# Windowed attention and a squared-ReLU MoE: reciprocals kept for a range test, with a second path behind a branch

## The chip, the core and the metric

The kernel runs on one core of a Trainium2 chip. The metric is the device time of one execution in microseconds; of a kernel several executions are timed, and the median is given. One further execution is recorded by the hardware profiler: its span runs from the first to the last instruction that the profile shows.

The engines are named as the profile names them: PE is TensorE (matrix multiplies; PEld its weight loads), DVE is VectorE, ACT is ScalarE, POOL is GpSimd and SP is SyncE. A "q" behind a name (SPq, ACTq) marks the engine's own sequencer: DMA issues, semaphore waits, drains. Each engine runs its own list of instructions in order; between engines they wait for each other through semaphores.

## The reference, cut to what matters

```python
# q, k, v: [8 batches, 8 heads, 576 positions, 64], float32, randn * 0.1
scores = scale * np.matmul(q, k.transpose(0, 1, 3, 2))        # scale = 1/8
mask = np.abs(pos[:, None] - pos[None, :]) <= 32
scores = np.where(mask, scores, -1e9)
scores = scores - np.max(scores, axis=-1, keepdims=True)
attn = np.exp(scores)
attn = attn / (np.sum(attn, axis=-1, keepdims=True) + 1e-09)
x = np.matmul(attn, v)          # heads side by side: [4608 tokens, 512]
r = np.maximum(x @ w_in, 0.0)   # w_in: [512, 2048]
out = (r * r) @ w_out           # w_out: [2048, 512]; out: [4608, 512] float32
```

## The kernel before, in words

The kernel works in bfloat16 with float32 accumulation, and it leaves out the row maximum: the exponentials are taken of the scores as they are.

*Tiles.* The 4608 tokens are cut into 24 groups G of 192 queries, three to a batch. A group has two halves, w = 0 (A) and w = 1 (B), each with 128 keys by 128 queries for 8 heads. `scores` (L565) puts transposed scores of one half into PSUM (`at`), ScalarE takes the exponential (L586, L589), VectorE multiplies by a mask of zeros and ones (L594). `pv` (L622) multiplies by v, which has a column of ones beside its 64 columns, so that column 64 of each head is the sum of the exponentials. On VectorE, the reciprocal of these sums (L641) goes into one of four small buffers `rs` (128 partitions by 8 heads), and a multiply (L644) with `rs` spread along 64 columns writes the normalised output into `xa` or `xb`. Half A uses partitions 64 to 127 alone, half B all 128. `xturn` transposes the outcome into `xt`: the first three groups on TensorE, the others by transposing DMAs that SyncE issues (L717, L720).

*MoE.* `mm1` (L737) multiplies `xt` with `w_in` into one of two PSUM tiles `ht`; ScalarE takes the relu (L743) into one of four buffers `rt`; VectorE squares (L746) into `gt`. `mm2` (L757) multiplies 128 tokens of `gt` with `w_out` into `outp`, ScalarE copies to `oe` (L767) and issues the store (L769). The last 128 tokens go in three column pieces (`mm2_last`, L782, L789, L792, L795); ScalarE issues two of their stores and SyncE one.

*Loads.* GpSimd issues the loads of q, k, v and the weights (L394, L426, L443, L456, L461), as they change type. Only the first two loads (L407) are SyncE's. In the opening TensorE fills its waits with multiplies of zeros (L322).

*What sets the order.* Nothing is issued as it is written. `Prog.rec` notes each operation with its engine, what it reads and writes, an estimated duration and a key; `Prog.schedule` simulates the engines with these durations and lets each engine take, of what is ready, the operation with the lowest key. `Prog.emit` writes the lists in the order found and adds a wait where an operation needs one of another engine, or an earlier result of its own. Operations of one engine that only reuse a buffer get no wait. Keys count steps of 64 tokens: group G has the keys 3G - 13 and a little more, `mm1` of tokens from t0 on has t0/64 to t0/64 + 8, `mm2` of block u has 2u + 9 to 2u + 10.5.

*The end.* `emit` runs in one block (L873). Behind the last operation SyncE waits for the landings of all stores (L877), and the block closes with a barrier of all engines: each drains and reports, GpSimd collects the reports and releases all.

The functions that the change touches:

Of the kernel before, what the change touches and what calls it, by code (L numbers as in the profile page):

```python
# [6 lines left out]
ACTF = mybir.ActivationFunctionType  # L7
BF16 = mybir.dt.bfloat16
F32 = mybir.dt.float32

B_, H_, S_, D_ = 8, 8, 576, 64
DM = 512
# [70 lines left out]
class Prog:  # L83
# [148 lines left out]
    def emit(self):  # L232
        nc = self.nc
        engs = {"PE": nc.tensor, "ACT": nc.scalar, "DVE": nc.vector, "POOL": nc.gpsimd, "SP": nc.sync}
        for op in self.ops:
            for d in op.deps:
                if d.dma is None and not (d.eng == "PE" and op.eng == "PE"):
                    d.inc = True
        sems = {e: nc.alloc_semaphore(f"s_{e}") for e in engs}
        count = {e: 0 for e in engs}  # L240
        dsems, dcount, total = {}, {}, {}
        for op in self.ops:
            if op.dma is not None:
                total[op.dma] = dcount[op.dma[0]] = dcount.get(op.dma[0], 0) + 16
        waited = {}
        for op in self.ops:
            e = engs[op.eng]
            need = {}
            for d in op.deps:
                if d.dma is None and d.eng == "PE" and op.eng == "PE":  # L250
                    continue
                need[d.sem] = max(need.get(d.sem, 0), d.val)
            for s, v in need.items():
                if waited.get((op.eng, s), 0) >= v:
                    continue
                waited[(op.eng, s)] = v
                e.wait_ge(sems[s] if s in sems else dsems[s], v)
            ins = op.fn(e)
            if op.dma is not None:
                s = op.dma[0]  # L260
                if s not in dsems:
                    dsems[s] = nc.alloc_semaphore(f"d_{s}")
                op.sem, op.val = s, total[op.dma]
                ins.then_inc(dsems[s], 16)
            elif op.inc:
                count[op.eng] += 1
                op.sem, op.val = op.eng, count[op.eng]
                ins.then_inc(sems[op.eng], 1)
        return dsems, dcount
# [10 lines left out]
class Gen:  # L280
# [5 lines left out]
    def alloc(self):  # L286
        nc = self.nc
        sb, ps = nc.alloc_sbuf_tensor, nc.alloc_psum_tensor
        self.AT = ps("at", [128, 2048], F32)
        self.HT = [ps(f"ht{i}", [128, 512], F32) for i in range(2)]  # L290
        self.OUTP = [ps(f"outp{i}", [128, 512], F32) for i in range(2)]

        self.RAW = {t: [sb(f"{t}raw{i}", [128, 2, 512], BF16) for i in range(NRAW)] for t in "qk"}
        self.QT = [sb(f"qt{i}", [128, 4, S_], BF16) for i in range(2)]
        self.KT = [sb(f"kt{i}", [128, 4, KW], BF16) for i in range(2)]
        self.V = [sb(f"v{i}", [128, 2, H_, VS], BF16) for i in range(NV)]
        self.DIF = sb("dif", [128, 128], F32)
        self.MASK = [sb(f"mask{i}", [128, 128], BF16) for i in range(4)]
        self.ID = sb("ident", [128, 128], BF16)
        self.E = [sb(f"e{i}", [128, 1024], BF16) for i in range(2)]  # L300
        self.PT = [sb(f"pt{i}", [128, 8, 128], BF16) for i in range(3)]
        self.RS = [sb(f"rs{i}", [128, 8], F32) for i in range(4)]
        self.XA = [sb(f"xa{i}", [128, 512], BF16) for i in range(3)]
        self.XB = [sb(f"xb{i}", [128, 512], BF16) for i in range(3)]
        self.XT = sb("xt", [128, 4, RING], BF16)
        self.W1 = sb("w1", [128, 4, DFF], BF16)
        self.W2 = sb("w2", [128, 16, DM], BF16)
        self.GT = sb("gt", [128, 16, RING], BF16)
        self.RT = [sb(f"rt{i}", [128, 512], BF16) for i in range(4)]
# [288 lines left out]
    def pv(self, G, w):  # L598
        b, g = divmod(G, 3)
        n = 2 * G + w  # L600
        key = 3 * G - LEAD + 0.3 * w + 0.1
        reg = 1 if NBIAS <= G < NSPLIT or G < NDUP and w else 0
        c0 = 1024 * reg
        vt, pt, avp = self.V[G % NV], self.PT[n % 3], self.AT
        hi, lo = [self.half(2 * reg, x) + self.half(2 * reg + 1, x) for x in (1, 0)]


        def f(e):
            if w and G < NDUP:
                for h in range(8):  # L610
                    x, y = divmod(h, 4)
                    c = c0 + 512 * x + 65 * y
                    e.matmul(avp[:, c:c + 65], self.PT[(n - 1) % 3][:, 4 * (h % 2) + h // 2, :], vt[:, 0, h, 0:65], start=(y == 0),
                             stop=True, skip_group_check=True)
            if w and G < NCLR:
                for x in range(2):
                    e.matmul(avp[64:128, c0 + 512 * x + 508:c0 + 512 * x + 512], self.ZZ[:, 0:64], self.ZZ[:, 0:4], start=True,
                             stop=True, skip_group_check=True)
            for h in range(8):
                x, y = divmod(h, 4)  # L620
                c = c0 + 512 * x + 65 * y
                mm = e.matmul(avp[:, c:c + 65], pt[:, 4 * (h % 2) + h // 2, :], vt[:, w, h, 0:65], start=(w == 0 and y == 0),  # L622
                              stop=True, skip_group_check=True)
            return mm

        rd = [("v", G % NV, w), ("vset", G % NV), ("pt", n % 3), "zz"]
        if G % 3 != 1:
            rd.append(("vpad", G % NV))
        if g and w == 0 and G < NVR:
            rd.append(("vl", G % NV))  # L630
        if G < NDUP and w:
            rd += [("pt", (n - 1) % 3), ("v", G % NV, 0)]
        self.p.rec("PE", f, reads=rd + (lo if w and G >= NDUP else []), writes=hi + lo, key=key, dur=260 + 160 * (w and G < NCLR) + 260 * (w and G < NDUP),
                   name=f"P{G}{'AB'[w]}")
        r0 = 64 * (1 - w)
        rs = self.RS[n % 4]
        x = (self.XB if w else self.XA)[G % 3]
        rd = hi + lo if w else hi
        av = avp[r0:128, c0:c0 + 1024].rearrange("p (x c) -> p x c", x=2)[:, :, 0:260].rearrange("p x (y c) -> p x y c", y=4)
        m = 128 - r0  # L640
        self.p.rec("DVE", lambda e: e.reciprocal(rs[r0:128, :].rearrange("p (x y) -> p x y", x=2), av[:, :, :, 64]),  # L641
                   reads=rd, writes=[("rs", n % 4)], key=key - 0.05, dur=190, name=f"R{G}{'AB'[w]}")
        rb = bass.AP(rs, r0 * 8, [[8, m], [4, 2], [1, 4], [0, 64]])
        self.p.rec("DVE", lambda e: e.tensor_tensor(x[r0:128, :].rearrange("p (x y c) -> p x y c", x=2, y=4),  # L644
                                                    av[:, :, :, 0:64], rb, ALU.mult),
                   reads=rd + [("rs", n % 4)], writes=[("xb" if w else "xa", G % 3)], key=key - 0.05,
                   dur=dve(512, False), name=f"N{G}{'AB'[w]}")
# [151 lines left out]
    def build(self):  # L799
# [37 lines left out]
        def at(key, f, *a):  # L837
            todo.append((key, len(todo), f, a))
# [20 lines left out]
        while t0 < NTOK:  # L859
            n = FIRST[t0] if t0 in FIRST else 192 if t0 < 768 else 256 if t0 < T512 else 512  # L860
            m = min(512 // n, 4)
            for d in range(0, 16, m):
                key = t0 / 64 + d / 16 * n / 64
                at(key, self.mm1, t0, n, list(range(d, d + m)), key)
            t0 += n
        at(500, self.mm2_last, NBLK - 1, 500)
        for u in range(NBLK - 1):
            for seg in range(4):
# [3 lines left out]
        p.schedule()  # L872
        with self.nc.Block():  # L873
            dsems, dcount = p.emit()
            for s in dsems:
                if s[0] == "o":
                    self.nc.sync.wait_ge(dsems[s], dcount[s])  # L877

    def opening(self):
        return OPENING  # L880


def bass_sliding_window_symmetric__then__act_relu_squared_kernel(nc, q, k, v, moe_w_in, moe_w_out, out):
# [29 lines left out]
```

## Time and profile before

| | |
|---|---|
| timed runs | 301.8, 302.01 and 302.15 us; median 302.01 us |
| profiled execution | span 299.9 us; a time of its own beside the span is not given |
| HBM | 36.70 MB read, 9.44 MB written |
| first matmul of the MoE (L737) in the span | 17.46 us |
| last reciprocal (L641) | 240.58 us |
| last matmul (L782) ends | 297.6 us |
| last store issued | 297.98 us |

How to read it: the page gives each engine's busy time, then the span in 40 slices with the busy share of each in tenths, the DMA queues, the chain of work that ended last, and groups of instructions. A group's row has line, engine, operation, output<-inputs, size and count, then its busy time and the mean in ns of one, then the idle time of the engine just before and what ended it. A row of the timeline has start in us, duration in us, engine, line and operation; in brackets stands the idle time before it and who ended it. A row for one line has the shortest, median and longest duration in ns and the first and last start in us.

### The profile page before, as it was taken

To read this page: it belongs to the slowest core of one execution; us is meant where nothing else is said; L and a number is where in the kernel's file an instruction comes from. 1 tells how busy PE (TensorE), PEld (TensorE's weight loads), DVE (VectorE), ACT (ScalarE), POOL (GpSimd) and SP (SyncE) were. 2 spreads that over 40 slices of the span, in tenths; PEclk is the share of its full clock that TensorE was granted. 3 is DMA by queue.
4 is the path that set the end of the run, shared out by engine and by line. 5 is a ranking of instruction groups with operands and counts; after the bars stand their busy time and mean duration, and the time that the engine had idled before them with its cause. 6 is when DMAs were issued, how large, how long until landed. Compare 5 with 4: busy or idle time off the path is not lost.

```text
span 299.9 us, 6209 instructions
## 1 busy us (share of the span) xinstructions
PE 291.9 (97%) x2394; PEld 171.8 (57%) x2431; DVE 167.2 (56%) x385; ACT 160.3 (53%) x250; POOL 107.1 (36%) x143
## 2 busy tenths in 40 slices
PE   7899999999999999999999999999999999999996
PEld 3578866848677767664544454444544444444445
DVE  6898775737674767563656666665666632222100
ACT  3497834836467656750765476536744643443312
POOL 8993336503544354455256335533500000000000
PEclk9999999999999999999999999999999999999999
DMA  9999999997999999999999999999992120100112
GB/s 169 176 206 184 196 177 174 169 176 137 164 169 165 95 162 146 155 138 186 180 168 131 114 166 156 125 149 156 154 128 70 55 61 35 37 35 35 38 70 105
DMA packets 160636, 39.83 MB, mean 133 GB/s; under 512 B 149984, under 2 KB 156128, under 8 KB 160608
## 3 DMA queue, kind: packets, MB, share of 16 engines
q0 software_dynamic: 106016, 17.93, 89.3%
q1 hardware_dynamic: 49264, 12.14, 28.5%
q10 hardware_dynamic: 5328, 9.37, 9.1%
q8 instruction: 19, 0.31, 0.5%
q14 instruction: 9, 0.07, 0.1%
HBM read 36.70 MB, written 9.44 MB: 154 GB/s over the span
## 4 chain that ended last, share of the span: by engine, by line
PE 90%; DMA 5%; POOL 3%; issue 1%; ACT 0%; POOLq 0%; ACTq 0%
PE ht L737 41%; PE outp L757 40%; DMA w<-in_moe_w_in_dram 5%; PE at L622 4%; PE at L565 4%; POOL v L443 1%; POOL w L456 1%; PE at L485 1%; PE ht L782 1%; PE outp L782 1%; POOL kpair L426 1%; POOL qpair L426 1%; ACT rt L743 0%; ACT oe L792 0%; POOL dif L325 0%
## 5 line engine op out<-in xcount | busy, mean ns | idle before, releaser
L737 PE MATMUL ht<-xt,w 128*128 128x256 bf16 (+2 forms) x885 | 140.0, 302 | 1.3 <-DMA w<-in_moe_w_in_dram 0.5
L757 PE MATMUL outp<-w,gt 128*128 128x512 bf16 x536 | 133.0, 379 | 1.3
L743 ACT ACTIVATE rt<-ht 128x512 bf16<-128x512 f32 (+1 forms) x152 | 85.9, 578 | 87.1 <-PE ht L737 85.1
L737 PEld LDWEIGHTS ht<-xt,w 128*128 128x128 bf16 x896 | 81.3, 98 | 43.8 <-ACT rt L743 0.6
L746 DVE TENSOR_TENSOR gt<-rt 128x512 bf16<-128x512 bf16 (+1 forms) x152 | 61.5, 408 | 61.6 <-ACT rt L743 60.0
L757 PEld LDWEIGHTS outp<-w,gt 128*128 128x128 bf16 x560 | 51.9, 98 | 54.1 <-ACT oe L767 1.0
L394 POOL DMA_DIRECT2D kraw<-in_k_dram x36 | 27.7, 778 | 107.3 <-PE at L622 56.8
L589 ACT ACTIVATE e<-at 128x1024 bf16<-128x1024 f32 x46 | 44.8, 1021 | 8.7 <-PE at L565 8.4
L594 DVE TENSOR_TENSOR pt<-e,mask 128x1024 bf16<-128x1024 bf16 x46 | 31.8, 691 | 29.0 <-ACT e L589 28.9
L443 POOL DMA_DIRECT2D v<-in_v_dram x48 | 38.2, 809 | 0.0
L767 ACT ACTIVATE oe<-outp 128x512 f32<-128x512 f32 x35 | 21.1, 604 | 29.6 <-PE outp L757 29.6
L394 POOL DMA_DIRECT2D qraw<-in_q_dram x36 | 27.7, 778 | 0.0
L622 PEld LDWEIGHTS at<-v,pt 128*128 128x128 bf16 x384 | 18.3, 98 | 9.9 <-DMA v<-in_v_dram 0.6
L622 PE MATMUL at<-v,pt 128*128 128x65 bf16 x384 | 20.1, 194 | 0.5 <-ACT pt L586 0.5
L644 DVE TENSOR_TENSOR xa<-at,rs 64x512 bf16<-64x512 f32 x24 | 16.7, 695 | 0.9
L644 DVE TENSOR_TENSOR xb<-at,rs 128x512 bf16<-128x512 f32 x24 | 16.5, 689 | 0.7
L565 PEld LDWEIGHTS at<-qt,kt 64*128 64x128 bf16 x384 | 10.8, 94 | 8.7 <-issue 7.1
L565 PE MATMUL at<-qt,kt 64*128 64x128 bf16 x384 | 15.2, 217 | 0.2
L641 DVE RECIPROCAL rs<-at 64x8 f32<-64x8 f32 (+1 forms) x48 | 10.0, 209 | 9.1 <-PE at L622 7.7
L650 DVE MEMSET at<- 64x520 f32 x23 | 11.3, 492 | 3.5 <-DVE xa L644 2.6
L450 DVE COPY v<-v 64x512 bf16<-64x512 bf16 x16 | 5.9, 372 | 5.1 <-PE ht L737 2.9
L789 DVE COPY oe<-ht 128x128 f32<-128x128 f32 x1 | 0.3, 292 | 14.5 <-PE ht L782 14.5
(67 smaller groups left out, 83.2 us busy)
## 6 DMA issues: line engine op xcount, KB each, us to landing
out_dram<-oe ACTq DMA_DIRECT2D x35, 256.0 KB, 3.2
qraw<-in_q_dram POOLq DMA_DIRECT2D x36, 96.0 KB, 5.8
w<-in_moe_w_in_dram POOLq DMA_DIRECT2D x4, 512.0 KB, 10.7
v<-in_v_dram POOLq DMA_DIRECT2D x16, 128.0 KB, 6.6
w<-in_moe_w_out_dram POOLq DMA_DIRECT2D x4, 512.0 KB, 18.8
v<-in_v_dram POOLq DMA_DIRECT2D x16, 96.0 KB, 7.0
kraw<-in_k_dram POOLq DMA_DIRECT2D x12, 112.0 KB, 4.6
kraw<-in_k_dram POOLq DMA_DIRECT2D x12, 96.0 KB, 4.9
```

Source lines behind the costliest of these rows:

```text
L394: self.p.rec("POOL", lambda e, j=j: e.dma_start(raw[0:h, j, :].rearrange("p (h d) -> p h d", h=8), s[:, j]), writes=[("raw", t, G % NRAW, ...
L443: self.p.rec("POOL", lambda e, j=j, lo=lo, hi=hi, k0=k0: e.dma_start(vt[lo - k0:hi - k0, j, :, 0:64], self.v[b, :, lo:hi, :].rearrange("h ...
L565: mm = e.matmul(sc[:, 512 * par + 128 * j:512 * par + 128 * j + 128], kt[r:r + 64, j, k0:k0 + 128], q, start=G >= NBIAS, stop=True, skip_g ...
L589: self.p.rec("ACT", lambda e, e_=e_, sc=sc: e.activation(e_[:], sc, ACTF.Exp, scale=0.125), reads=tags[w], writes=[("e", n % 2)], key=key, ...
L594: self.p.rec("DVE", lambda e, pt=pt, ee=ee, mb=mb: e.tensor_tensor(pt[:], ee, mb, ALU.mult), reads=[("e", n % 2), ("mask", mi)], writes=[( ...
L622: mm = e.matmul(avp[:, c:c + 65], pt[:, 4 * (h % 2) + h // 2, :], vt[:, w, h, 0:65], start=(w == 0 and y == 0), stop=True, skip_group_chec ...
L644: self.p.rec("DVE", lambda e: e.tensor_tensor(x[r0:128, :].rearrange("p (x y c) -> p x y c", x=2, y=4), av[:, :, :, 0:64], rb, ALU.mult), ...
L737: mm = e.matmul(ht[:, n * x:n * x + n], self.W1[:, ft, 128 * d:128 * d + 128], self.XT[:, ft, r:r + n], start=(ft == 0), stop=(ft == 3))
L743: self.p.rec("ACT", lambda e: e.activation(rt[:, 0:c], ht[:, 0:c], ACTF.Relu), reads=[f"ht{k % 2}"], writes=[("rt", k % 4)], key=key, dur= ...
L746: self.p.rec("DVE", lambda e: e.tensor_tensor(gt[:, d0:d0 + len(ds), r:r + n], rr, rr, ALU.mult), reads=[("rt", k % 4)], writes=[("gt", s, ...
L757: mm = e.matmul(op[:], gt[:, d, r:r + 128], self.W2[:, d, :], start=(d == 0), stop=(d == 15))
L767: self.p.rec("ACT", lambda e: e.activation(oe, op[:], ACTF.Copy), reads=[f"outp{u % 2}"], writes=[("oe", u % 4)], key=key, dur=act(512), n ...
```

## The change

The four buffers `rs` become one tensor `rsa` with a place of its own for each of the 48 halves. A memset fills what half A does not write (partitions 0 to 63) with ones. Behind the last half, VectorE tests all 384 values of each partition against 2^-40 and 2^40 and takes the minimum; SyncE moves the 128 minima into one partition by a DMA; VectorE takes their minimum and writes a flag (0 or 1). At the end of the block all five engines wait for that instruction, load the flag into a register, and behind the barrier each compares it with 0. If it isn't 0, they enter `General`, a second path: float32 attention with row maxima in loops over batch, head and 96 queries, written to `out`, and then the MoE from `out` in a loop over 36 blocks. If it is 0, they jump over that path, which stands last in the program.

The diff, with the second path cut to its head:

```diff
-        sems = {e: nc.alloc_semaphore(f"s_{e}") for e in engs}
+        sems = self.sems = {e: nc.alloc_semaphore(f"s_{e}") for e in engs}
...
-        self.RS = [sb(f"rs{i}", [128, 8], F32) for i in range(4)]
+        self.RSA = sb("rsa", [128, 2 * NG, 8], F32)
+        self.OK = sb("ok", [128, 2 * NG * 8], F32)
+        self.OKP = sb("okp", [128, 1], F32)
+        self.OKR = sb("okr", [1, 128], F32)
+        self.OK1 = sb("okmin", [1, 1], F32)
+        self.FLAG = sb("flag", [1, 1], I32)
...
-        rs = self.RS[n % 4]
+        rs = self.RSA[:, n, :]
...
-        self.p.rec("DVE", lambda e: e.reciprocal(rs[r0:128, :].rearrange("p (x y) -> p x y", x=2), av[:, :, :, 64]),
-                   reads=rd, writes=[("rs", n % 4)], key=key - 0.05, dur=190, name=f"R{G}{'AB'[w]}")
-        rb = bass.AP(rs, r0 * 8, [[8, m], [4, 2], [1, 4], [0, 64]])
+        self.p.rec("DVE", lambda e: e.reciprocal(rs[r0:128].rearrange("p (x y) -> p x y", x=2), av[:, :, :, 64]),
+                   reads=rd, writes=[("rs", n)], key=key - 0.05, dur=190, name=f"R{G}{'AB'[w]}")
+        rb = bass.AP(self.RSA, (r0 * 2 * NG + n) * 8, [[16 * NG, m], [4, 2], [1, 4], [0, 64]])
...
+        self.range_ones()
+        at(3 * NG, self.range_flag)
...
             dsems, dcount = p.emit()
+            for e in (self.nc.tensor, self.nc.scalar, self.nc.vector, self.nc.gpsimd, self.nc.sync):
+                e.wait_ge(p.sems["DVE"], self.flagged.val)
+            off = self.nc.values_load(self.FLAG[:], min_val=0, max_val=1, ...)
             for s in dsems:
                 if s[0] == "o":
                     self.nc.sync.wait_ge(dsems[s], dcount[s])
+        with self.nc.If(off != 0):
+            General(self).build()
+
+    def range_ones(self):
+        ones = self.RSA[0:64].rearrange("p (g w) h -> p g w h", w=2)[:, :, 0, :]
+        self.p.rec("DVE", lambda e: e.memset(ones, 1.0), writes=["rsones"], key=6, dur=350, name="rsones")
+
+    def range_flag(self):
+        p, rsa = self.p, self.RSA[:].rearrange("p n h -> p (n h)")
+        key = 3 * NG
+        p.rec("DVE", lambda e: e.tensor_scalar(self.OK[:], rsa, 2.0 ** -40, None, ALU.is_ge),
+              reads=["rsones"] + [("rs", n) for n in range(2 * NG)], writes=["ok0"], key=key, dur=560, name="okge")
+        p.rec("DVE", lambda e: e.scalar_tensor_tensor(self.OK[:], rsa, 2.0 ** 40, self.OK[:], ALU.is_le, ALU.mult),
+              reads=["ok0"], writes=["ok1"], key=key, dur=560, name="okle")
+        p.rec("DVE", lambda e: e.tensor_reduce(self.OKP[:], self.OK[:], mybir.AxisListType.X, ALU.min),
+              reads=["ok1"], writes=["okp"], key=key, dur=560, name="okmin")
+        p.rec("SP", lambda e: e.dma_start(self.OKR[:], self.OKP[:]), reads=["okp"], writes=["okr"], dma=("ok", 0), key=key,
+              dur=600, move=(1, 100), name="okdma")
+        p.rec("DVE", lambda e: e.tensor_reduce(self.OK1[:], self.OKR[:], mybir.AxisListType.X, ALU.min),
+              reads=["okr"], writes=["ok2"], key=key, dur=250, name="okrow")
+        self.flagged = p.rec("DVE", lambda e: e.tensor_scalar(self.FLAG[:], self.OK1[:], 0.5, None, ALU.is_lt),
+                             reads=["ok2"], writes=["flag"], key=key, dur=100, name="flag")
+        self.flagged.inc = True
...
+class General:
+    def do(self, e, f, inc=1):
+        if self.n:
+            e.wait_ge(self.sem, self.n)
+        f(e).then_inc(self.sem, inc)
+        self.n += inc
...
+        with nc.Fori(0, B_) as b:
+            with nc.Fori(0, H_) as h:
...
+                with nc.Fori(0, N) as c:
...
+        with nc.Fori(0, NBLK) as t:
...
```

The lists of the changed program hold, on VectorE, the memset between the copy of `kt` (L516, 768 elements) and the first reciprocal, then the two tests and the reduction around the first square (L746) behind the last multiply (L644), and the last two instructions behind three more squares. On SyncE the DMA stands between the last transpose and the store of L795. The register loads stand behind each engine's last operation, on SyncE ahead of the waits of L877.

More of the change, by code (lines that the diff above doesn't have):

```diff
@@ L9 @@
 F32 = mybir.dt.float32
+I32 = mybir.dt.int32
 B_, H_, S_, D_ = 8, 8, 576, 64
@@ L640, in pv @@
         m = 128 - r0
-        self.p.rec("DVE", lambda e: e.reciprocal(rs[r0:128, :].rearrange("p (x y) -> p x y", x=2), av[:, :, :, 64]),
-                   reads=rd, writes=[("rs", n % 4)], key=key - 0.05, dur=190, name=f"R{G}{'AB'[w]}")
-        rb = bass.AP(rs, r0 * 8, [[8, m], [4, 2], [1, 4], [0, 64]])
+        self.p.rec("DVE", lambda e: e.reciprocal(rs[r0:128].rearrange("p (x y) -> p x y", x=2), av[:, :, :, 64]),
+                   reads=rd, writes=[("rs", n)], key=key - 0.05, dur=190, name=f"R{G}{'AB'[w]}")
+        rb = bass.AP(self.RSA, (r0 * 2 * NG + n) * 8, [[16 * NG, m], [4, 2], [1, 4], [0, 64]])
         self.p.rec("DVE", lambda e: e.tensor_tensor(x[r0:128, :].rearrange("p (x y c) -> p x y c", x=2, y=4),
                                                     av[:, :, :, 0:64], rb, ALU.mult),
-                   reads=rd + [("rs", n % 4)], writes=[("xb" if w else "xa", G % 3)], key=key - 0.05,
+                   reads=rd + [("rs", n)], writes=[("xb" if w else "xa", G % 3)], key=key - 0.05,
                    dur=dve(512, False), name=f"N{G}{'AB'[w]}")
@@ L874, in build @@
             dsems, dcount = p.emit()
+            for e in (self.nc.tensor, self.nc.scalar, self.nc.vector, self.nc.gpsimd, self.nc.sync):
+                e.wait_ge(p.sems["DVE"], self.flagged.val)
+            off = self.nc.values_load(self.FLAG[:], min_val=0, max_val=1, skip_runtime_bounds_check_because="a comparison wrote it")
             for s in dsems:
```

111 lines of the change are left out of this document (added).

## The prediction

> **What bounds the kernel now.** I read the page's span, busy times and slices first, then the chain of work that ended last, then the stretches that the change touches: the opening, the stretch behind the last reciprocal, and the end.
>
> ```profile
> span 299.9 us, 6209 instructions
> PE 291.9 (97%) x2394; PEld 171.8 (57%) x2431; DVE 167.2 (56%) x385; ACT 160.3 (53%) x250; POOL 107.1 (36%) x143
> ...
> PE   7899999999999999999999999999999999999996
> ...
> PEclk9999999999999999999999999999999999999999
> ```
>
> TensorE is busy for 291.9 of 299.9 us at the full clock in every slice; only the first slice and the last have gaps. VectorE, which gets nearly all of the added work, is busy for 56%. So an edit costs time in three cases: it makes TensorE wait, it delays the opening, or it lengthens what follows the last matmul. The profile gives the execution's span, 299.9 us; the three timed runs have a median of 302.01 us, so 2.1 us lie around the span. I take these as unchanged.
>
> The chain, as shares of the span, and its part from 9 to 26 us (start, us, what):
>
> ```profile
> PE 90%; DMA 5%; POOL 3%; issue 1%; ACT 0%; POOLq 0%; ACTq 0%
> ```
>
> ```profile
> 10.19 13.79 DMA w<-in_moe_w_in_dram
> 23.98 0.14 issue
> 24.11 1.48 PE ht L737 x16
> ```
>
> The opening is not set by VectorE: up to 23.98 us the chain hangs on one weight load (L456), and TensorE starts its MoE work at 24.11 when that has landed. From there on the chain is TensorE itself.
>
> **The change, part by part.** The order of the changed program, engine by engine, is that of the program before, except for these additions. VectorE gets one memset, three instructions over 384 elements and two over 128 and 1 elements; SyncE gets one DMA; every engine gets a wait, a load of one register and a branch at its end. The instructions that follow the branch are the second path, which is not to be executed.
>
> *The reciprocals' new place.* The 48 reciprocals and 48 multiplies keep size and order. The four small buffers of before were written and read by VectorE alone, so no semaphore of another engine goes away and none comes. Cost 0, for and against. The larger tiles push the tensors allocated behind them up by 3,552 bytes; shapes and strides stay, so 0 here too.
>
> *The memset of ones* (192 elements on 64 partitions) stands on VectorE between the eviction of kt and the first reciprocal:
>
> ```profile
> 10.67 1.02 DVE L516 COPY kt<-outp 128x768 bf16<-128x768 bf16 x1 [0.25 <-PE outp L485]
> 11.72 0.21 DVE L641 RECIPROCAL rs<-at 64x8 f32<-64x8 f32 x1
> ...
> 12.58 0.69 DVE L644 TENSOR_TENSOR xa<-at,rs 64x512 bf16<-64x512 f32 x1
> ```
>
> ```profile
> 13.33 0.29 PE L671 MATMUL ht<-ident,xa 64*128 64x64 bf16 x4 [0.44 <-DVE xa L644]
> ...
> 24.11 1.48 PE L737 MATMUL ht<-xt,w 128*128 128x192 bf16 x16 [0.47 <-DMA w<-in_moe_w_in_dram]
> ```
>
> Prices of the nearest forms, from the groups by form (busy us, mean ns of one):
>
> ```profile
> L316 DVE MEMSET zz<- 128x256 uint32 x1 | 0.3, 272 | 0.9 <-PEq L898 0.9
> L316 DVE MEMSET kt<- 128x64 uint32 x4 | 0.4, 112 | 0.0
> L333 DVE TENSOR_SCALAR ident<-dif 128x128 bf16<-128x128 f32 x1 | 0.1, 150 | 0.0
> L348 DVE SCALAR_TENSOR_TENSOR mask<-dif,mask 128x64 bf16<-128x64 f32 x4 | 0.9, 222 | 0.0
> L644 DVE TENSOR_TENSOR xb<-at,rs 128x512 bf16<-128x512 f32 x24 | 16.5, 689 | 0.7
> ```
>
> 64 elements take 112 ns and 256 take 272, so 192 take about 0.22 us by the straight line between them. VectorE is dense there, and TensorE waits 0.44 us for xa (L671), so the 0.22 us pass to TensorE at 13.33. At 24.11 TensorE waits 0.47 us for the weights, whose DMA does not depend on this. The delay ends in that wait: 0.22 is under 0.47. I take 0; without that cover the memset costs 0.22 us.
>
> *The test.* These are the rows of VectorE and SyncE behind the last multiply:
>
> ```profile
> 240.82 0.69 DVE L644 TENSOR_TENSOR xb<-at,rs 128x512 bf16<-128x512 f32 x1
> ...
> 241.59 1.19 SPq L720 DMA_TRANSPOSE xt<-xb  x1
> ...
> 242.05 0.43 DVE L746 TENSOR_TENSOR gt<-rt 128x512 bf16<-128x512 bf16 x1 [0.53 <-ACT rt L743]
> ...
> 243.77 0.42 DVE L746 TENSOR_TENSOR gt<-rt 128x512 bf16<-128x512 bf16 x1 [1.30 <-ACT rt L743]
> ...
> 247.23 0.42 DVE L746 TENSOR_TENSOR gt<-rt 128x512 bf16<-128x512 bf16 x1 [1.04 <-ACT rt L743]
> ...
> 248.95 0.42 DVE L746 TENSOR_TENSOR gt<-rt 128x512 bf16<-128x512 bf16 x1 [1.30 <-ACT rt L743]
> ```
>
> No row has 384 float32 elements, nor a reduction. The lower end is 0.15 us (128 elements, L333). The upper end is 1.3 us (the 222 ns that L348 takes for 64 elements, six times). I take 0.5 each, near the 689 ns that L644 takes for 512 elements. The first test fits between 241.51 and 242.05, the second and the reduction (1.0 us) between 242.48 and 243.77. At the upper end the square at 243.77 starts some 2 us late. Behind a late square wait ScalarE's relu, which needs the rt buffer back four squares later (about 6.9 us), and the second matmul, whose keys lie 1.5 steps of 64 tokens behind the last first matmul of its tokens. Both cover 2 us. Cost 0.
>
> The DMA of 128 words waits for the reduction, on SyncE, behind the last transpose (L720) and ahead of one store at 297 us. VectorE's next added instruction waits for its landing, after the third square (247.65 us). Issued near 243.6 it lands after 1.6 us (the 64 KB store further down), or after 7.4 us, the most that this queue's transposes took:
>
> ```profile
> DMA to landing us min/median/max: 2.3/3.9/7.4
> ```
>
> That is 245 to 251 us. At worst VectorE stands still from 247.65 to 251, and the squares of 248.95 and 250.7 come 2 us late, which the same two reserves cover. Cost 0.
>
> *The end.* The last two stores are issued, SyncE waits for the landings (L877), and a barrier (L873) closes the block:
>
> ```profile
> 297.04 0.38 SPq L795 DMA_DIRECT2D out_dram<-oe  x1
> ...
> 297.98 0.34 ACTq L795 DMA_DIRECT2D out_dram<-oe  x1
> ```
>
> ```profile
> L877 SPq EVENT_SEMAPHORE  x4: 17/28/28, 297.5 to 299.6; - x4
> ```
>
> ```profile
> L873 POOLq EVENT_SEMAPHORE  x2: 17/17/17, 299.7 to 299.7; - x2
> ...
> L873 ACTq DRAIN  x1: 153/153/153, 298.4 to 298.4; - x1
> L873 SPq DRAIN  x1: 7/7/7, 299.6 to 299.6; - x1
> ...
> L873 PEldq EVENT_SEMAPHORE  x1: 51/51/51, 299.8 to 299.8; - x1
> ```
>
> The wait for the flag was met 45 us earlier: nothing. The register load stands ahead of the barrier on all engines, and on SyncE ahead of its waits. SyncE has from 297.42 to 299.6 for it, 2.2 us. ScalarE has least: its issue ends at 298.32, its drain takes 0.15, the barrier is reached at 299.6: 1.1 us. No row shows a register load. From below it is a semaphore step, 17 ns; from above a whole 64 KB store from issue to landing:
>
> ```profile
> out_dram<-oe ACTq DMA_DIRECT2D x1, 64.0 KB, 1.6
> ```
>
> At 1.6 us ScalarE would be 0.5 us late. One word is far nearer to the lower end in work, so I take a load under 1.1 us, hidden in the last store's flight: 0, with 0.5 kept as the upper end. [...]
>
> The branch stands behind the barrier on all engines at once, with nothing beside it. A step of a sequencer takes 17 to 51 ns in the rows above; a compare and a jump are a few such steps, so I take 0.15 us. The other end is the code load below.
>
> The sum: 299.9 + 0 (place) + 0 (memset) + 0 (test) + 0 (load) + 0.15 (branch) + 2.1 around it = 302.15, told as **302.2 us**. Alone this case has 301.8 to 302.6: the spread of the timed runs below, memset and most of the load above.
>
> **The rivals.**
>
> *The jump has to load code* (slower). The taken path jumps over the second path. Instructions come by DMA:
>
> ```profile
> q8 instruction: 19, 0.31, 0.5%
> q14 instruction: 9, 0.07, 0.1%
> ```
>
> A packet of q8 is 16 KB, one of q14 8 KB. TensorE has some 4,830 rows (2,394 and 2,431) for 19 packets of q8, that is about 254 instructions of 64 bytes each, so q14's packets have about 125. By the built program the jump passes some 45 instructions on ScalarE, 50 on SyncE and GpSimd, 64 on VectorE and about 250 on TensorE: less than one packet each, so the target lies in the block in use or in the next. In favour of a hit: the code is fetched ahead, as TensorE's chain with 1% "issue" shows. Against: whether a jump uses the block fetched ahead no row of this trace shows. It decides from the point where one engine's target is not there. The price: a packet of q8 takes 0.5% of 16 x 299.9 us / 19 = 1.3 us, one of q14 0.5 us, and a landing 1.6 us: 2.1 to 2.9 us, so 304.1 to 304.9. [...]
>
> *The load is not hidden on ScalarE* (slower). Where it takes 1.6 to 2.3 us, the barrier starts 0.5 to 1.2 us later: 302.6 to 303.3. For it: the load stands right behind ScalarE's last issue. Against: only 1.1 us are to be filled by one word.
>
> *The test takes the second path.* Each reciprocal is of a sum of 33 to 65 exponentials of small scores, far inside the limits 2^-40 and 2^40; the unwritten half is filled with ones. 384 rounds of the second path, with two DMAs of at least 1.6 us in each, would be over 1,200 us longer.
>
> *Faster.* No wait or instruction goes away; only a changed alignment of transfers in the opening could gain, and the chain shows one load that the change does not touch.
>
> **How the numbers follow.** Forecast 0.61; code load 0.19; load on ScalarE 0.15; faster 0.04; second path 0.01. The range runs from 301.7 to 304.6: all of the forecast and of the late load, and about two thirds of the code load; some 0.1 is left out. A measurement of this kernel can tell about 0.2% (0.6 us) from no change. Slower by more: the code load, the late load but for its lower edge and the second path, 0.34. Faster by more: 0.03. Within: 0.63.
>
> **What would show it.** Right: in the changed profile the first reciprocal starts some 0.2 us later, TensorE still waits for the weights at 24.1 us and for no VectorE instruction after 240 us, the squares keep their 1.7 us beat, SyncE's waits and not ScalarE's load end last before the barrier, and the span ends 0.1 to 0.3 us after it. Wrong: a gap of 2 us or more behind the barrier (code load), ScalarE's drain after 299.6 us (load), TensorE idle near 245 to 260 us (test), or the start of L737 moved past 24.3 us (memset).

## The result and the profile after

The changed kernel takes 302.5 us (median of 18 runs, 302.21 to 302.91), the kernel before 302.07 us (18 runs beside them, 301.68 to 302.44). The ratio is 1.0016, with an interval of 1.0009 to 1.0022: slower by 0.43 us. That is a difference, though it is under the 0.2% that the prediction called the bound of what can be told. In the profiled execution the span grew from 299.9 to 300.4 us.

The code moved down by six lines and more: L641 is now L647, L644 is L650, L737 is L743, L746 is L752, L782 is L788, L873 is L881, L877 is L888. The register load is L885. The branch is recorded under a line of a helper, bacc.py:44.

From the page of the changed kernel, in the order span, busy times, code queues (packets, MB, share of the 16 DMA engines' time):

```profile
span 300.4 us, 6230 instructions
...
PE 292.4 (97%) x2394; PEld 171.7 (57%) x2431; DVE 168.1 (56%) x391; ACT 160.3 (53%) x250; POOL 106.8 (36%) x143
...
q8 instruction: 19, 0.31, 0.5%
q14 instruction: 9, 0.07, 0.1%
```

TensorE has the same matmuls and the same 97%. VectorE has six more instructions, and still 56%. The code queues fetched no more packets within the span than before. TensorE got no work, though its busy time is 0.5 us longer, and its last matmul ends at 297.79 us where it ended at 297.58 before. That is no more than executions differ by: in the profiles of the ten kernels below this end lies between 297.52 and 298.05 us, and it is earliest in the one that has all the tests and no branch (e1).

**The opening.** The timeline of VectorE, then of TensorE (start, duration, line, idle time before and who ended it):

```profile
8.05 1.14 DVE L522 COPY kt<-outp 128x896 bf16<-128x896 bf16 x1
...
9.27 0.22 DVE L894 MEMSET rsa<- 64x192 f32 x1
...
10.45 1.02 DVE L522 COPY kt<-outp 128x768 bf16<-128x768 bf16 x1 [0.18 <-PE outp L491]
11.49 0.21 DVE L647 RECIPROCAL rsa<-at 64x8 f32<-64x8 f32 x1
```

```profile
13.17 0.29 PE L677 MATMUL ht<-ident,xa 64*128 64x64 bf16 x4 [0.52 <-DVE xa L650]
...
24.14 0.49 PE L743 MATMUL ht<-xt,w 128*128 128x192 bf16 x4
```

The memset takes the forecast 0.22 us, but it does not stand between the 768-element eviction of kt and the first reciprocal, as the prediction and the account of the change have it: it runs behind the 896-element one, ahead of 0.18 us in which VectorE waits anyway. The first reciprocal comes at 11.49 us, not 0.2 us later than the 11.72 of before but 0.23 earlier; in the other profiles that have the memset it starts anywhere between 11.59 and 12.29 us. The matmul that began at 24.11 us begins at 24.14, here without a wait for weights. In most of the profiles below that have the memset (e2, e3, e5 to e10) TensorE does wait for the weights there, for 0.23 to 0.70 us.

**The tests.** VectorE behind the last multiply, then SyncE's DMA in its timeline, and in the list of DMA issues (KB, us from issue to landing):

```profile
240.89 0.69 DVE L650 TENSOR_TENSOR xb<-at,rsa 128x512 bf16<-128x512 f32 x1
241.50 0.35 DVE L900 TENSOR_SCALAR ok<-rsa 128x384 f32<-128x384 f32 x1
242.15 0.43 DVE L752 TENSOR_TENSOR gt<-rt 128x512 bf16<-128x512 bf16 x1 [0.29 <-ACT rt L749]
242.49 0.55 DVE L902 SCALAR_TENSOR_TENSOR ok<-rsa,ok 128x384 f32<-128x384 f32 x1
243.07 0.55 DVE L904 TENSOR_REDUCE okp<-ok 128x1 f32<-128x384 f32 x1
243.93 0.42 DVE L752 TENSOR_TENSOR gt<-rt 128x512 bf16<-128x512 bf16 x1 [0.30 <-ACT rt L749]
...
247.38 0.42 DVE L752 TENSOR_TENSOR gt<-rt 128x512 bf16<-128x512 bf16 x1 [1.16 <-ACT rt L749]
247.73 0.27 DVE L908 TENSOR_REDUCE okmin<-okr 1x1 f32<-1x128 f32 x1
248.03 0.14 DVE L910 TENSOR_SCALAR flag<-okmin 1x1 int32<-1x1 f32 x1
249.11 0.43 DVE L752 TENSOR_TENSOR gt<-rt 128x512 bf16<-128x512 bf16 x1 [0.94 <-ACT rt L749]
```

```profile
243.65 0.56 SPq L906 DMA_DIRECT2D okr<-okp  x1
```

```profile
okr<-okp SPq DMA_DIRECT2D x1, 0.5 KB, 2.0
```

The brackets carry the reading: each square still waits for ScalarE's relu, and none starts late because of a test. The tests fill idle time that stands smaller in the brackets: 0.29, 0.30 and 0.94 us, where before it was 0.53, 1.30 and 1.30. The DMA landed 2.0 us after its issue at 243.65, two microseconds before VectorE came to need it. TensorE waits for nothing on VectorE behind 240 us.

**The end.** Register loads (L885), then SyncE's waits for the stores, the barrier, and the branches, each row with the shortest, median and longest duration in ns and the first and last start in us:

```profile
L885 POOLq TENSOR_LOAD <-flag x1: 498/498/498, 248.2 to 248.2; - x1
L885 PEldq TENSOR_LOAD <-flag x1: 490/490/490, 296.6 to 296.6; - x1
L885 DVEq TENSOR_LOAD <-flag x1: 628/628/628, 297.1 to 297.1; - x1
L885 SPq TENSOR_LOAD <-flag x1: 518/518/518, 297.8 to 297.8; - x1
L885 ACTq TENSOR_LOAD <-flag x1: 481/481/481, 298.5 to 298.5; - x1
```

```profile
L888 SPq EVENT_SEMAPHORE  x4: 28/28/28, 298.4 to 299.7; - x4
```

```profile
L881 ACTq DRAIN  x1: 8/8/8, 299.0 to 299.0; - x1
L881 SPq DRAIN  x1: 7/7/7, 299.8 to 299.8; - x1
...
L881 PEldq EVENT_SEMAPHORE  x1: 51/51/51, 300.0 to 300.0; - x1
```

```profile
bacc.py:44 POOLq COMPARE_BRANCH  x1: 50/50/50, 300.0 to 300.0; - x1
bacc.py:44 ACTq COMPARE_BRANCH  x1: 54/54/54, 300.0 to 300.0; - x1
bacc.py:44 SPq COMPARE_BRANCH  x1: 53/53/53, 300.0 to 300.0; - x1
bacc.py:44 DVEq COMPARE_BRANCH  x1: 72/72/72, 300.1 to 300.1; - x1
bacc.py:44 PEldq COMPARE_BRANCH  x1: 344/344/344, 300.1 to 300.1; - x1
```

ScalarE is at its drain at 299.0 us, 0.8 us ahead of SyncE's, which follows the last landing: the load is hidden. Before, the span ended with the barrier, whose last row began at 299.8 and took 51 ns. Now the last of the barrier's rows begins at 300.0, and behind it stand the branches. Four engines need 50 to 72 ns. TensorE needs 344 ns, and its end is the end of the span. Unrounded in the trace, the barrier is over at 300.007 and the span at 300.449 us: 0.44 us behind the barrier, where before there was nothing. Before, barrier and span ended at 299.850. So of the 0.60 us between the two profiled executions, 0.44 lie behind the barrier; the other 0.16 come from ahead of it, from TensorE's later end told above.

### The profile page after: what moved, and what is told of

It is laid out like the page before. It is cut to its first block, busy times and chain, and to the rows that moved or that the text cites. A ratio compares the mean times of both kernels' runs of the same rounds, so it can differ in the third digit from the quotient of the medians.

```text
span 300.4 us, 6230 instructions
## 1 busy us (share of the span) xinstructions
PE 292.4 (97%) x2394; PEld 171.7 (57%) x2431; DVE 168.1 (56%) x391; ACT 160.3 (53%) x250; POOL 106.8 (36%) x143
## 4 chain that ended last, share of the span: by engine, by line
PE 93%; DMA 3%; POOL 2%; issue 1%; DVE 1%; ACT 0%; POOLq 0%
PE ht L743 42%; PE outp L763 40%; PE at L571 4%; PE at L628 4%; DMA qpair<-in_q_dram 3%; POOL v L449 1%; PE at L491 1%; PE ht L788 1%; PE outp L788 1%; POOL kpair L432 0%; POOL w L462 0%; POOL qpair L432 0%; DVE xb L650 0%; DVE qraw L435 0%; ACT rt L749 0%
## 5 line engine op out<-in xcount | busy, mean ns | idle before, releaser
L743 PE MATMUL ht<-xt,w 128*128 128x256 bf16 (+2 forms) x885 | 140.0, 302 | 0.9 <-ACT rt L749 0.2
L743 PEld LDWEIGHTS ht<-xt,w 128*128 128x128 bf16 x896 | 81.3, 98 | 43.6 <-ACT rt L749 0.3
L752 DVE TENSOR_TENSOR gt<-rt 128x512 bf16<-128x512 bf16 (+1 forms) x152 | 61.6, 409 | 59.8 <-ACT rt L749 58.2
L650 DVE TENSOR_TENSOR xa<-at,rsa 64x512 bf16<-64x512 f32 x24 | 16.7, 695 | 1.0
L650 DVE TENSOR_TENSOR xb<-at,rsa 128x512 bf16<-128x512 f32 x24 | 16.6, 690 | 0.9
L647 DVE RECIPROCAL rsa<-at 64x8 f32<-64x8 f32 (+1 forms) x48 | 10.1, 209 | 9.0 <-PE at L628 7.4
L328 PE MATMUL outp<-zz 128*128 128x512 bf16 x23 | 7.6, 470 | 1.2 <-DVE zz L322 1.2
```

The source lines that it names most:

```text
L743: mm = e.matmul(ht[:, n * x:n * x + n], self.W1[:, ft, 128 * d:128 * d + 128], self.XT[:, ft, r:r + n], start=(ft == 0), stop=(ft == 3))
L752: self.p.rec("DVE", lambda e: e.tensor_tensor(gt[:, d0:d0 + len(ds), r:r + n], rr, rr, ALU.mult), reads=[("rt", k % 4)], writes=[("gt", s, ...
```

## The experiments

The theory (A), which the runs bear out only in part: the whole loss is the branch behind the barrier, and TensorE's above all; tests and loads are hidden. Rivals: the tests or the memset cost something (B), the loads do (C). Then, of TensorE's branch: is its price that of loading code (D)? In all of these kernels the first path computes everything; what differs is the test, the load, the branch or what is skipped. A rival that no kernel here takes up is the reciprocals' new place, which all of them keep. e1 to e10 were timed in five rounds beside the kernel before (302.02 to 302.06 us), with 11 runs each, but 4 of e7 and 5 of e8 and e10; the first row is the result above. The ratios are estimates of their own, not quotients of the medians.

The recorded expectations have letters of their own. In e1 to e4 and e8, J is A here, K is B with the opening, L is C. In e5 to e7, C is the code load (D here), D a price that goes with the distance of the jump, F a fixed price. In e9, A and B are E and F, which come up below, and A1 and A2 in e10 are two forms of E.

| kernel | time, us | ratio | interval | span, median of its runs | TensorE's branch, ns |
|---|---|---|---|---|---|
| changed kernel | 302.5 | 1.0016 | 1.0009 to 1.0022 | 300.55 | 344 |
| e1_tests_only | 302.25 | 1.0006 | 0.9996 to 1.0015 | 300.1 | none |
| e2_loads | 302.27 | 1.0009 | 0.9996 to 1.0021 | 300.2 | none |
| e3_small_body | 302.2 | 1.0000 | 0.9991 to 1.0009 | 300.2 | none |
| e4_no_tests | 302.52 | 1.0017 | 1.0008 to 1.0026 | 300.6 | 344 |
| e5_one_each | 302.4 | 1.0008 | 0.9999 to 1.0017 | 300.5 | 215 |
| e6_te_130 | 302.48 | 1.0009 | 0.9996 to 1.0021 | 300.6 | 344 |
| e7_te_600 | 305.55 | 1.0114 | 1.0098 to 1.0129 | 303.6 | 3594 |
| e8_early_branch | 303.73 | 1.0049 | 1.0035 to 1.0062 | 301.9 | 350 |
| e9_early_short | 302.31 | 1.0007 | 0.9998 to 1.0016 | 300.2 | 220 |
| e10_early_te_130 | 303.49 | 1.0047 | 1.0034 to 1.0061 | 301.3 | 344 |

The kernel before has a median span of 300.0 us in the runs beside e1 to e10.

**Tests alone.** Memset, tests and DMA stay; the flag is written and not used.

```diff
-            for e in (self.nc.tensor, self.nc.scalar, self.nc.vector, self.nc.gpsimd, self.nc.sync):
-                e.wait_ge(p.sems["DVE"], self.flagged.val)
-            off = self.nc.values_load(self.FLAG[:], ...)
...
-        with self.nc.If(off != 0):
-            General(self).build()
```

> Memset, tests, DMA and flag are kept; the waits, the register loads, the branch and the second path are left out. Theory J (the cost lies behind the barrier: the compare and jump, 0.44 us of span there in the changed kernel's trace, 0.34 of it on TensorE): ratio to before 1.000 (302.0 to 302.2 us), span 299.9 to 300.1, nothing behind the barrier. Theory K (the cost lies in VectorE's added work and in the opening, where TensorE ended 0.2 us later): ratio 1.0010 to 1.0016.

Measured: 1.0006, and no difference from the kernel before that the interval tells from nothing. The span ends with the barrier again, at 299.8 us in the profiled execution. Alone this leaves B up to 0.45 us (0.0015 of 302); e4 closes more of it.

**Loads without a branch.** Only the branch and the second path are gone.

```diff
-        with self.nc.If(off != 0):
-            General(self).build()
```

> As the changed kernel, but without the branch and the second path; the flag is loaded on all five engines and not used. J: as the run with the tests alone, ratio 1.000, since the load (0.48 us on ScalarE in the changed kernel's trace) ends 0.7 us before the last store has landed. A third theory, L (the loads cost): ratio 1.001 or more, and ScalarE's drain reaches the barrier last.

Measured: 1.0009, with an interval from 0.9996. But this kernel did not do what it was made for: the value, which nothing uses, was not loaded; the trace shows on L885 three waits of 17 to 51 ns and no register load. It tests the waits alone, and says nothing on C.

**A small second path.** One memset on VectorE in place of the second path.

```diff
         with self.nc.If(off != 0):
-            General(self).build()
+            self.nc.vector.memset(self.OKP[:], 0.0)
```

> As the changed kernel, but the second path is one memset on VectorE: the branch is there and jumps over next to nothing; the second path's work is left out. J in the form that the price goes with the distance of the jump: TensorE's branch falls from 0.34 us to the 0.05 to 0.07 of the other engines, the span ends 0.15 us behind the barrier in place of 0.44, ratio 1.0003 to 1.0008. J in the form that a branch on TensorE costs this much anyway: 0.34 us again, ratio 1.0010 to 1.0016. K: ratio 1.0010 to 1.0016 with nothing behind the barrier to show for it.

Measured: 1.0000. This one missed its aim too, and in an instructive way. Its only branch is this:

```profile
bacc.py:44 DVEq COMPARE_BRANCH  x1: 72/72/72, 299.9 to 299.9; - x1
```

The four engines that have nothing to do in this second path got neither the load nor the branch: the only register load on L885 is VectorE's, of 675 ns. So it shows what the branch costs if TensorE hasn't one: a row of 72 ns that ends the span 0.12 us behind the barrier, and no difference in time that the interval tells from nothing.

**No tests.** The flag is set by a memset in the opening; loads, branch and the whole second path stay.

```diff
-        self.range_ones()
-        at(3 * NG, self.range_flag)
+        self.flagged = self.p.rec("DVE", lambda e: e.memset(self.FLAG[:], 0), writes=["flag"], key=6, dur=100, name="flag")
+        self.flagged.inc = True
```

> The branch, the loads and the whole second path are kept, but the flag is a constant zero written early by VectorE: memset of ones, tests, reduction and DMA are left out, and with them the check of the range. J: ratio as the changed kernel's, 1.0010 to 1.0020, TensorE's branch 0.34 us. K: ratio 1.000 to 1.0006.

Measured: 1.0017, the changed kernel's 1.0016. Without any test the loss is all there. So B isn't needed for it: memset, tests and DMA together cost nothing that shows against this kernel.

**One instruction on each engine in the second path**, so that all five have the branch, but jump over two instructions each:

```diff
-            General(self).build()
+            sem = self.nc.alloc_semaphore("few")
+            for i in range(1):
+                self.nc.tensor.matmul(self.OUTP[1][:], self.ZZ[:, 0:128], self.ZZ[:], start=True, stop=True)
+            self.nc.scalar.activation(self.RT[0][:, 0:8], self.ZZ[:, 0:8], ACTF.Copy)
+            self.nc.vector.memset(self.OKP[:], 0.0)
+            self.nc.gpsimd.memset(self.DIF[:, 0:8], 0.0)
+            self.nc.sync.dma_start(self.OKR[:], self.RSA[0:1, 0:16, :].rearrange("p n h -> p (n h)")).then_inc(sem, 16)
+            self.nc.sync.wait_ge(sem, 16)
```

> As the changed kernel, but the second path is one instruction on each engine (and one on TensorE is a multiply of zeros): all five engines branch, and jump over one or two instructions; the second path's work is left out. Distance theory D (TensorE's 0.34 us are the price of a long jump): all five branches 0.05 to 0.08 us, the span ends 0.15 us behind the barrier, ratio 1.0003 to 1.0009. Fixed-price theory F (a branch on TensorE costs 0.34 us whatever the distance): 0.34 us again, ratio 1.0010 to 1.0020.

Measured: 1.0008 [0.9999, 1.0017]. The row that moved is TensorE's; the other four stand as in the changed kernel:

```profile
bacc.py:44 PEldq COMPARE_BRANCH  x1: 215/215/215, 300.2 to 300.2; - x1
```

So most of TensorE's branch is there with nearly nothing to jump over: neither the 50 to 80 ns of a price by distance nor the 340 of a fixed one. The time of this kernel lies between those without a branch on TensorE and the changed one, but the intervals overlap with both.

**130 and 600 multiplies** on TensorE in the skipped path, the other engines as in e5. A multiply is a weight load and a matmul, two rows in the trace. By the prediction's 254 instructions to a block of 16 KB, 130 are about one block and 600 nearly five. Against e5 (e7 has 600 in place of 130):

```diff
-            for i in range(1):
+            for i in range(130):
                 self.nc.tensor.matmul(self.OUTP[1][:], self.ZZ[:, 0:128], self.ZZ[:], start=True, stop=True)
```

> The same with 130 multiplies of zeros on TensorE in the path that is jumped over (about 260 instructions with their weight loads, near the changed kernel's 250), one instruction on each other engine; the second path's work is left out. D: TensorE's branch 0.3 to 0.4 us, ratio 1.0010 to 1.0020. F: the same. Code-load theory C, that TensorE's target lies in a block that has not come: 1.5 us or more.

> The same with 600 multiplies of zeros on TensorE in the path that is jumped over (at least 600, with weight loads 1,200 instructions, several blocks of 256); the second path's work is left out. C: the target can't have come, TensorE waits for its code 2 to 3 us behind the barrier, ratio 1.006 to 1.010. F: 0.34 us, ratio 1.0010 to 1.0020. D without a code load: between 0.34 and 1.5 us.

Measured: 130 multiplies give TensorE's branch the 344 ns that the real second path gives it, and 1.0009 [0.9996, 1.0021], a ratio that alone can't be told from that of a kernel without the branch. 600 give 1.0114, above the 1.006 to 1.010 that were expected, and these rows, the branch and the code queue within the span:

```profile
bacc.py:44 PEldq COMPARE_BRANCH  x1: 3594/3594/3594, 299.9 to 299.9; - x1
```

```profile
q8 instruction: 20, 0.33, 0.5%
```

The twentieth block of code starts 1.0 us into the branch, at 300.92 us, and the engine stands for 3.6 us. This is what loading code looks like, and what the prediction's first rival described with 2.1 to 2.9 us. In the changed kernel the branch takes a tenth of it, and its code fetches come behind the span, from 301.06 us on. D falls for the changed kernel and holds for a longer jump. The jump over nearly five blocks stalls (3,594 ns), the one over about a block does not (344 ns). No run has a jump between the two, so where the stall begins was not shown.

**The branch early.** If the branch is the loss, it can be hidden: it may stand ahead of SyncE's waits, while the last stores are in flight. The second path then begins with these waits and a barrier of its own.

```diff
+            with self.nc.If(off != 0):
+                for s in dsems:
+                    if s[0] == "o":
+                        self.nc.sync.wait_ge(dsems[s], dcount[s])
+                self.nc.all_engine_barrier()
+                General(self).build()
             for s in dsems:
                 if s[0] == "o":
                     self.nc.sync.wait_ge(dsems[s], dcount[s])
-        with self.nc.If(off != 0):
-            General(self).build()
```

> The whole change with its second path, but the branch stands ahead of SyncE's waits for the stores and of the block's barrier; the second path begins with these waits and a barrier of its own. J (the cost lies in what follows the barrier): TensorE's 0.34 us and the others' 0.05 lie in the 1.7 us that the last store is in flight, the span ends with the barrier as before, ratio 1.000 to 1.0006. Theory K (opening, tests): ratio as the changed kernel's, 1.0010 to 1.0020.

Measured: 1.0049, worse than the change itself. The branches were hidden (TensorE's 350 ns at 297.5, ScalarE's, the last, at 299.3 us), but the last two stores landed late. The code queues and the list of DMA issues (KB each, median us from issue to landing):

```profile
q8 instruction: 20, 0.33, 0.5%
q14 instruction: 12, 0.10, 0.1%
...
out_dram<-oe SPq DMA_DIRECT2D x1, 64.0 KB, 3.4
out_dram<-oe ACTq DMA_DIRECT2D x1, 64.0 KB, 2.7
```

Both stores take 1.6 us in the kernel before and in the changed one. Four blocks of code more lie within the span, one of 16 KB and three of 8 KB; one of the latter comes at 250 us, long before the stores. The landing of each of these stores stands in the trace in 16 parts; in the kernel before and in the changed one the 16 lie within 0.20 us. Of SyncE's here, 15 were in by 299.14 us and one came at 300.93; of ScalarE's, 14 were in by 299.92 and two came at 300.61 and 301.11. A new theory (E): the blocks fetched behind a jump hold up single parts of stores in flight. Its rival (F): a load or a branch ahead of the waits costs it, whatever is fetched.

**The branch early, with a short path**, and the same with 130 multiplies on TensorE. Both are e8 with the second path of e5 and of e6 in place of its own (e10 has 130 in place of 1):

```diff
-                self.nc.all_engine_barrier()
-                General(self).build()
+                sem = self.nc.alloc_semaphore("few")
+                for i in range(1):
+                    self.nc.tensor.matmul(self.OUTP[1][:], self.ZZ[:, 0:128], self.ZZ[:], start=True, stop=True)
+                self.nc.scalar.activation(self.RT[0][:, 0:8], self.ZZ[:, 0:8], ACTF.Copy)
...
```

> The branch stands where e8 put it, ahead of SyncE's waits for the stores and ahead of the barrier; the second path is one instruction on each engine in place of float32 attention and the MoE, so a jump hardly leaves the block of code at hand. Theory A (e8's 1.0049 came from the blocks of code that were fetched after its jumps, which held up single packets of the last two stores): no block of 8 or 16 KB is fetched between 297.5 and 299.7 us, all 16 partial landings of each of the last two stores come within 0.3 us of each other, TensorE's branch of 0.2 to 0.35 us lies ahead of the barrier, the span ends with the barrier and is 299.8 to 300.2 us; ratio 0.999 to 1.001. Theory B (e8's loss came from branches or loads ahead of the waits as such, not from code): ratio 1.003 to 1.006 as in e8, with late landings again.

> As e9_early_short, but with 130 multiplies on TensorE in the skipped path and one instruction on each other engine: only TensorE's jump is long enough to bring a new block of 16 KB into play, as in e6. Theory A1 (TensorE's 16 KB block alone holds up the stores): one 16 KB block is fetched between 297.5 and 299.9 us, single packets of the last two stores land over 0.5 us behind their fellows, ratio 1.002 to 1.005. Theory A2 (the 8 KB blocks of the other engines held them up in e8): the 16 KB block is fetched but the landings stay within 0.3 us, or one packet of SyncE's store alone is late and the end is set by ScalarE's store as before: ratio under 1.0015.

Measured: e9 1.0007 [0.9998, 1.0016], e10 1.0047 [1.0034, 1.0061]. The code queue and the last stores of e9, then of e10:

```profile
q8 instruction: 19, 0.31, 0.5%
...
out_dram<-oe SPq DMA_DIRECT2D x1, 64.0 KB, 1.6
out_dram<-oe ACTq DMA_DIRECT2D x1, 64.0 KB, 1.6
```

```profile
q8 instruction: 20, 0.33, 0.5%
...
out_dram<-oe SPq DMA_DIRECT2D x1, 64.0 KB, 3.2
out_dram<-oe ACTq DMA_DIRECT2D x1, 64.0 KB, 2.5
```

The two differ in 129 multiplies that are never executed. With them TensorE fetches one block of 16 KB, from 298.44 to 299.59 us, and of each store one part of 16 comes late: SyncE's at 300.67, 1.56 us behind the other 15, ScalarE's at 300.84, 1.0 us behind them. E holds and F falls: e9 has all loads and branches ahead of the waits and loses nothing against e1. The single DMA packets of e10's trace show the order. In each store the late part is eight packets of 512 bytes. SyncE's eight start at 299.58 us, when the block of code ends, and ScalarE's at 300.03, when SyncE's have gone. In e8 the order is the same: the block of 16 KB ends at 299.85 us, SyncE's late eight start at 299.84 and eight of ScalarE's at 300.29; its other late eight start at 299.72, as a block of 8 KB ends (299.73). As for C, loads and branches that are hidden cost nothing that the intervals show.

**All runs together.** Each interval above is about as wide as the loss, and together the runs say less for A than e4 alone. The four kernels without a branch of TensorE behind the barrier (e1, e2, e3, e9; 44 runs) take on average 0.17 us more than the kernel before beside them, 0.05 to 0.30 when the runs are resampled. The three in which that branch takes 344 ns (the changed kernel, e4, e6; 40 runs) take 0.40 us more, 0.30 to 0.50. So about 0.23 us of the loss, 0.06 to 0.39, goes with TensorE's branch, about half of it. What the rest goes with stays open. The tests are not shown to be it, as e4 loses no less without them, and no kernel was built without the reciprocals' new place.

## Why the prediction was right, point by point

The forecast was 302.2 us, a change within 0.2%; 302.5 us and 0.16% were measured. The tests and the loads, which the prediction took as hidden, are hidden in the trace, and one term, the branch, was too small. That the number held is in part the width of the range, 0.4 us to either side. Of the signs named, three did not come: the later reciprocal, the wait for weights at 24.1 us, and an end 0.1 to 0.3 us behind the barrier. By its steps:

- *The reciprocals' new place, 0; the memset, 0.* Right in cost as far as single intervals tell: tests, memset and new place together are in e1, at 1.0006 with 1 inside the interval, and e4 has the full loss without memset and tests; by all runs together 0.17 us are open, which the new place could hold. The memset's 0.22 us was exact. Its place was wrong, and so was the sign that was to show it, a reciprocal 0.2 us later. The wait for weights that was to cover it is not there in the profiled execution of the changed kernel, but it is in eight other profiles with the memset; that the memset needs that cover was not shown by any run.
- *The tests, 0.5 us each, 0 on the path.* 0.35, 0.55 and 0.55 us, and the DMA 2.0 us in a range of 1.6 to 7.4. All of it fits between the squares, as the step said, and TensorE waits for none of it.
- *The register load, under 1.1 us and hidden.* 0.48 to 0.63 us, with 0.8 us to spare on ScalarE. Four of the five rows lie at 0.48 to 0.52, VectorE's at 0.63.
- *The branch, 0.15 us on all engines at once.* This is the term that was mis-sized. It was made of sequencer steps of 17 to 51 ns, and for four engines that is right (50 to 72 ns). TensorE was taken as one engine among the five; its branch takes 344 ns, it starts 0.1 us behind the barrier's end, and the sum is 0.44 us of the span. In the time it is less: about 0.23 us by all runs together.
- *2.1 us around the span, unchanged.* Nearly: the median of what lies around the span is 2.03 us in the runs of the kernel before and 1.92 in those of the changed one. The spans grew by 0.55 us, the time by 0.43. The other kernels split alike: 1.92 to 1.96 us around the span in those with a branch behind the barrier (e3 to e7), 2.07 to 2.17 in e1, e2, e9 and e10, where the span ends with the barrier; only e8, with 1.79, doesn't fit. So some 0.1 us of what a branch adds to the span is not added to the time; why was not tried.
- *The rivals.* The code load isn't what happened, but it is real: e7 pays 3.6 us, more than the 2.1 to 2.9 that were worked out from a packet and a landing. The load on ScalarE did not come, and the second path was not entered.

The forecast's own range, 301.8 to 302.6 us, held the time. With the branch at the price in the trace the sum would be 299.9 + 0.44 + 2.1 = 302.4, a small loss in place of nearly none.

## What to carry to other kernels

The branch behind the last barrier had nothing to hide behind, and its slowest engine ended the span: four engines were done in 50 to 72 ns, TensorE took 344, and the span ended 0.44 us behind the barrier, against 0.12 where VectorE alone had a branch (e3). So bound such a step engine by engine, and give a branch only to engines that need one. Work that fits into the idle time of an engine off the path (five instructions of 0.14 to 0.55 us and a DMA of 2.0 us for the tests here) made TensorE wait for nothing behind 240 us. Before moving a branch under a last transfer, count the code that it jumps over. With two instructions on TensorE (e9) no block was fetched before the stores had landed; with about a block (e10) 16 KB were fetched behind the jump, the last two stores landed 3.2 and 2.5 us after their issue in place of 1.6, and the time was 1.0047 of the kernel before, more than the 0.23 us that went with the branch. Between the two nothing was measured. And where single intervals are as wide as the effect, take the runs of all related kernels together before calling a cause the whole of it.

## What the runs showed of the hardware that was not expected

- The branch over the second path takes 50 to 72 ns on GpSimd, ScalarE, SyncE and VectorE (the changed kernel, e4, e5, e7), and on TensorE 215 to 220 ns over two instructions (e5, e9), 344 to 350 over about 250 (the changed kernel, e4, e6, e8, e10), and 3,594 ns over about 1,200 (e7), where a block of code is fetched from 1.0 us into the branch. Why TensorE needs 130 ns more for 250 instructions than for two was not settled; it does so behind the barrier (e5, e6) and ahead of it (e9, e10).
- One block of 16 KB fetched while two 64 KB stores were in flight (e10) left 15 of each store's 16 parts on time and held one up, by 1.56 us in SyncE's store and by 1.0 in ScalarE's. In e8, with two blocks of 8 KB beside it, one part of SyncE's store was 1.8 us late and two of ScalarE's 0.7 and 1.2 us. SyncE's late packets start as the block ends (299.58 against 299.59 us in e10, 299.84 against 299.85 in e8). Why they start then was not shown.
